# Attention into top-1 experts: min and exp of each step ranked first, row scatters declared independent

## The chip, the cores and the metric

The kernel runs on one core of a Trainium2 chip. The metric is the device time of one execution in microseconds (us), lower is better, median of several runs.

## What is computed

Two stages stand one behind the other. The first is attention with rotary embedding over 4 batches and 8 heads, 576 positions, head size 64. The second is a layer of 8 experts over the 2304 rows of 512 that the attention leaves; every row goes to one expert. Which expert it is hangs on the row before: where the local gate is at least one half, the row takes over the expert of its predecessor.

```python
def _attn_ref(q, k, v):
    q_rot, k_rot = (rotate(q), rotate(k))
    scores = scale * np.matmul(q_rot, k_rot.transpose(0, 1, 3, 2))
    scores = scores - np.max(scores, axis=-1, keepdims=True)
    attn = np.exp(scores)
    attn = attn / (np.sum(attn, axis=-1, keepdims=True) + 1e-09)
    return np.matmul(attn, v).astype(np.float32)

def _moe_ref(x, w_gate, w_local, w1, w2):
    ...
            fresh_e = int(np.argmax(logits[b, s]))
            if s == 0 or local_gate[b, s] < 0.5:
                e = fresh_e
            else:
                e = prev_e if prev_e >= 0 else fresh_e
            ...
            h = np.maximum(x[b, s] @ w1[e], 0.0)
            out[b, s] = p[e] * (h @ w2[e])
```

## The kernel before, in words

**Tiling.** Two heads make a pair, so there are 16 pairs; each pair is cut into 9 steps of 128 queries against 576 keys, and one loop runs over the 144 steps g. Step 9p is pair p's first. From pair 2 on the first step of a pair is the tail tile, which holds the last 64 queries of both heads (its exp writes a tile `et`; the others write `e`). Products that need fp32 are made of two fp32r parts: a high part, cast by ACT, and a low part, the rest, by DVE.

**One step.** The loop's body writes, for step g: the minimum over the scores (`softmax_min`, L269, on DVE: `mn<-s`); the scores of the next step (`mm_s(g + 1)`, L264, on PE); the exp (`softmax_exp`, L286, on ACT: `e<-s,mn` or `et<-s,mn`, with the row sums); the transposes of step g-2 (`tr_main`: PE `tm` L322, two of nine steps also `tk` L332, the tail also `tt` L338), whose result ACT casts (`pth<-tm`, `pkh`, L300) and DVE subtracts (`ptl<-tm,pth`, `pkl`, L304); up to five matmuls of step g-11's product with v (`pv`, L358), whose result is taken out by ACT (`tmp<-pv`, L368) and DVE (`xt<-pv,tmp`, L369). Rope and splits of later pairs go to POOL and the DMA queues. From pair 2 on the gates of a finished pair (PE `gx` L433, DVE `gm` L441 and `xrow` L443) and, around pairs 13 to 15, the routing of three batches (many short operations on DVE: `mx`, `rs`, `d`, `c8`, `key` ...) lie among the steps.

**What is shared.** The scores have two PSUM buffers, so `mm_s(g)` waits until the exp of step g-2 has read its buffer. One pool of four PSUM buffers holds `tm`, `tk`, `tt`, `pv`, `gx` and the small tiles of the routing. The normalising sums are set at a batch's turn (L423, L426).

**What sets the order.** Each step is a region of its own: within it the first 12 steps keep every engine in the order of the code, later steps only PE. How the instructions of neighbouring regions fall among one another, and everything on DVE, ACT, POOL and SP from step 12 on, is the scheduler's choice, which takes the ready instruction with the smallest rank. Behind the loop comes a drain whose order is written out by hand, and then the experts.

**The experts.** 19 tiles of 128 rows run, one behind the other: gather of rows (POOL), transposes, first product (`h`, L918), relu, transposes, second product (`o`, L940), scaling by ACT (`os<-o,x`, L945) and a scatter of the 128 rows to their places in the output, issued by POOL (L946). The scatters go to the same output tensor, and each waits until the one before has landed. Behind the last scatter the program only waits for its landing.

The loop's head is:

```python
                mn = softmax_min(g)
                if g + 1 < NSTEP:
                    mm_s(g + 1)
                softmax_exp(g, mn)
                if g >= 2:
                    tr_main(g - 2)
                pv_steps(g - 11)
```

Of the kernel before, what the change touches and what calls it, by code (L numbers as in the profile page):

```python
# [37 lines left out]
MAN1 = None  # L38
MAN2 = {mybir.EngineType.PE, mybir.EngineType.DVE}
MAN0 = {PE_}  # L40
LOAD0 = 4
ON_POOL = (125, 129, 130, 132, 134)
DRAIN = "tPststatbgttttwtguttegSuuuxXGGGSS"
# [92 lines left out]
def tile_attention_moe(ctx, tc, qk, v, tabs, turn, consts, tri, wg, wts, out):  # L136
    nc = tc.nc
    pe, act, dve, pool, sp = nc.tensor, nc.scalar, nc.vector, nc.gpsimd, nc.sync
# [94 lines left out]
    def spread(p):  # L233
        spread_tail(p)
        spread_k(p)
        spread_q(p)

    def heads_of(i):
        return (i % 2, i // 2)

    def tile_of(g):

        p, i = divmod(g, 9)
        return p, i if p < 2 else (i + 8) % 9

    def mm_s(g):
        p, i = tile_of(g)
        m, q = m_t[p], qst[p % 2]
        st = ps_s.tile([P, 2, 512], F32, tag="s", name=f"s_{g}")
        whole = [(h, 0, HALF, h * HALF) for h in range(2)]  # L250

        turned = [(0, 0, HALF, 64), (1, 0, 224, 64 + HALF), (1, 224, HALF, 0)]
        if i < 8:
            a, j = heads_of(i)
            seq = [(q[:, a, j * P:(j + 1) * P], m[:, a, c], whole) for c in range(2)]
        elif p > 1:
            qt, k = qtail[p % 2], xk[p % 2]
            seq = [(qt[:, x], k[:, y], whole) for x, y in PASSES]
        else:
            seq = [(qtail0[p][:, a], m[:, a, c], (whole, turned)[a]) for a in range(2) for c in range(2)]  # L260
        for h in range(2):
            parts_ = [(lhs, keys, lo, hi, k0) for lhs, keys, parts in seq for hh, lo, hi, k0 in parts if hh == h]
            for n, (lhs, keys, lo, hi, k0) in enumerate(parts_):
                pe.matmul(st[:, h, lo:hi], lhs, keys[:, k0:k0 + hi - lo], start=(n == 0), stop=(n == len(parts_) - 1))  # L264
        s_t[g] = st

    def softmax_min(g):
        mn = sm_p.tile([P, 1], F32, tag="mn", name=f"mn_{g}", bufs=4)
        dve.tensor_reduce(mn, s_t[g][:, :, 0:HALF], axis=AX.XY, op=ALU.min)  # L269
        return mn  # L270

    def softmax_exp(g, mn):
        p, i = tile_of(g)
        b, hp = divmod(p, NP)
        sums = sum_t[b]
        if i < 8:
            a, j = heads_of(i)
            if a == 0:
                e_t[p, j] = ej_p.tile([P, 2, S], F32, tag="ej", name=f"e_{p}_{j}")
            dst = e_t[p, j][:, a]  # L280
            col = (2 * hp + a) * NB + j
        else:
            e_t[p, 4] = et_p.tile([P, S], F32, tag="et", name=f"et_{p}")
            dst = e_t[p, 4]
            col = 2 * hp * NB + 4
        act.activation(  # L286
            dst.rearrange("p (h s) -> p h s", h=2), s_t.pop(g)[:, :, 0:HALF], AF.Exp,
            bias=mn, scale=-1.0, accum_out=sums[:, col:col + 1],
        )
# [414 lines left out]
    def early():  # L704
# [45 lines left out]
        def load_more():  # L750
            for k in range(2, LOAD0):
                load_w(0, k)
            yield
# [65 lines left out]
    def load_w(t, k):  # L819

        if t in regs:
            e, need = regs[t]
            if k == 7 and not w_stage:
                w_stage.append(over.tile([P, 2 * S], F32, tag="xk1", name="stage_7"))
            cols = slice(k * 1024, (k + 1) * 1024)
            sp.dma_start(staged(k), wts[bass.ds(e, 1), :, cols], cond=need)
# [108 lines left out]
    def second_product(t):  # L935
        ps = ps_t.tile([P, 512], F32, tag="t", name=f"o_{t}")
        for k in range(8):
            w = w_t[t, 4 + k // 2]
            for n, (x, y) in enumerate(PASSES):
                pe.matmul(ps, hs_t[t][:, x, k], w[y][:, (k % 2) * 512:(k % 2 + 1) * 512],  # L940
                          start=(k == 0 and n == 0), stop=(k == 7 and n == 2))
            if k % 2 == 1:
                yield k
        o = et_p.tile([P, S], F32, tag="et", name=f"os_{t}")
        act.activation(o[:, 0:DM], ps, AF.Copy, scale=x_t[t][:, DM:DM + 1])  # L945
        pool.indirect_dma_start(  # L946
            out=outf, out_offset=bass.IndirectOffsetOnAxis(ap=sidx[:, t:t + 1], axis=0),
            in_=o[:, 0:DM], in_offset=None, bounds_check=NT - 1, oob_is_err=False)

    LAST = KE + U_LATE - 1  # L950

    def experts_phase():
# [33 lines left out]
        for _ in second_product(LAST):  # L986
            yield LAST
# [122 lines left out]
    if True:  # L1110
# [39 lines left out]
        for g in range(NSTEP):  # L1150
            if g == GM:
                begin.close()
            with tc.manual_schedule(engines=None if g < GM else MAN0):
                p, i = divmod(g, 9)
                if i == 0 and p % NP == 0:
                    b = p // NP
                    sum_t[b] = sm_p.tile([P, H * NB], F32, tag="sum", name=f"sum_{b}")
                    dve.memset(sum_t[b], 1.0)
                mn = softmax_min(g)
                if g + 1 < NSTEP:  # L1160
                    mm_s(g + 1)
                softmax_exp(g, mn)
                if g >= 2:
                    tr_main(g - 2)
                pv_steps(g - 11)

                if i == 0 and 2 <= p and p + 2 < NPAIR or g == SPREAD_LAST:
                    spread(p + 1)
                if g in START:
                    for f in START[g]:  # L1170
                        f()
                if i == 0 and 1 <= p and p + 2 < NPAIR:
                    rope(p + 2)
                    if p + 3 < NPAIR:
                        load_qk(p + 3)
                if i == 5 and 1 <= p and p + 3 < NPAIR:
                    split_qk(p + 2)
                if g == QK_LAST:
                    split_qk(NPAIR - 1)
                if i == 3 and 1 <= p and p + 1 < NPAIR:  # L1180
                    split_v(p + 1)
                    if p + 2 < NPAIR:
                        load_v(p + 2)

                if i == GATES_AT.get(p, 7) and p >= 2:
                    soon += gates(p - 2)
                    if (p - 2) % NP == NP - 1:
                        soon.append(lambda b=(p - 2) // NP: scores(b))
                        if (p - 2) // NP == B - 2:
                            todo += route(0, B - 1)  # L1190
                if soon:
                    soon.pop(0)()
                f = todo.pop(0) if todo else None
                if f:
                    list(f())
        moe = experts_phase()
        with tc.manual_schedule(engines=MAN1):
# [20 lines left out]
            def rest_of_w():  # L1218
                for k in range(LOAD0, 8):
                    load_w(0, k)  # L1220
# [81 lines left out]
```

## Time and profile before

| what | value |
|---|---|
| time, median of 3 runs | 553.76 us (553.4 to 555.82) |
| the profiled execution, its own time | 553.2 us |
| its span, first to last instruction | 551.0 us |
| mean granted TensorE clock | 0.993 |
| PE, matmuls | 525.8 us busy (95%) |
| PE, weight loads | 465.9 us busy (85%) |
| DVE | 383.7 us busy (70%) |
| ACT | 339.5 us busy (62%) |
| POOL | 326.4 us busy (59%) |

The page gives busy time over the whole span. The stages differ: the attention runs from about 13 to 294 us, the drain to about 320, the experts to 540, and the rest is the last scatter and the end of the program. What a stage is bound by is read from its own stretch. In a row of the timeline the first number is the start, the second the length; the bracket at the end gives the idle time of that engine just before the row and what ended it.

### The profile page before, as it was taken

What the parts mean: (1) busy time and instruction counts of PE and PEld (TensorE: products, weight loads), DVE (VectorE), ACT (ScalarE), POOL (GpSimd) and SP (SyncE); (2) the same over time, 40 slices, a digit from 0 to 9 for tenths busy, and PEclk for the clock granted to TensorE, in tenths of its full rate; (3) what the DMA queues carried; (4) which work ended last, traced back from release to release, by engine and by line L of the source; (5) the groups of instructions that cost most, each with busy time, mean ns of one, the idle gap of its engine ahead of it and who ended that gap; (6) DMA issues with size and microseconds to landing.
All of it is one profiled execution on the core that took longest, in us unless ns stands there. A gap on an engine that the chain in (4) does not pass through costs nothing. (4 is left out here: it accounts for less than half of the span.)

```text
span 551.0 us, 10813 instructions
## 1 busy us (share of the span) xinstructions
PE 525.8 (95%) x3328; PEld 465.9 (85%) x3329; DVE 383.7 (70%) x723; ACT 339.5 (62%) x755; POOL 326.4 (59%) x243
## 2 busy tenths in 40 slices
PE   7989999999999999998999999999999999999991
PEld 3788999999999999997888788887888888888881
DVE  5898999999999999999999746356411545312530
ACT  2989889888998999987667424252422344423340
POOL 2995988989778788985698202265312444411331
PEclk9999999999999999999999999999999999999997
DMA  8558597886787787886298224644215464215140
GB/s 282 217 117 214 176 252 204 188 228 191 215 229 176 202 229 208 216 199 160 29 187 239 68 50 143 207 176 163 69 39 204 131 259 167 82 39 192 58 136 24
DMA packets 48774, 90.46 MB, mean 164 GB/s; under 512 B 15233, under 2 KB 25473, under 8 KB 46914
## 3 DMA queue, kind: packets, MB, share of 16 engines
q1 hardware_dynamic: 45666, 79.96, 51.2%
q0 software_dynamic: 3040, 9.71, 5.5%
q8 instruction: 29, 0.48, 0.4%
q14 instruction: 39, 0.32, 0.2%
HBM read 109.95 MB, written 9.71 MB: 217 GB/s over the span
## 5 line engine op out<-in xcount | busy, mean ns | idle before, releaser
L940 PE MATMUL o<-w,hs 128*128 128x512 f32 x456 | 113.1, 398 | 0.0
L269 DVE TENSOR_REDUCE mn<-s 128x1 f32<-128x576 f32 x144 | 107.4, 746 | 4.2 <-PE s L264 2.7
L918 PE MATMUL h<-w,xs 128*128 128x512 f32 x444 | 106.1, 392 | 0.8 <-DVE xs L304 0.5
L286 ACT ACTIVATE e<-s,mn 128x576 f32<-128x576 f32 x128 | 95.3, 745 | 17.3 <-DVE mn L269 14.3
L264 PE MATMUL s<-m,qst 128*128 128x288 f32 x512 | 97.6, 311 | 5.9 <-ACT e L286 3.7
L946 POOL DMA_INDIRECT out_dram<-os,sidx x19 | 22.8, 1198 | 132.2 <-ACT os L945 84.4
L304 DVE TENSOR_TENSOR ptl<-tm,pth 128x512 fp32r<-128x512 f32 x139 | 95.0, 684 | 6.3 <-ACT pth L300 4.1
L918 PEld LDWEIGHTS h<-w,xs 128*128 128x128 f32 x444 | 82.5, 188 | 19.0 <-DVE w L866 1.1
L940 PEld LDWEIGHTS o<-w,hs 128*128 128x128 f32 x456 | 83.1, 188 | 16.9 <-DVE hs L304 0.4
L300 ACT CAST pth<-tm 128x512 fp32r<-128x512 f32 x139 | 81.0, 582 | 12.9 <-PE tm L322 12.0
L264 PEld LDWEIGHTS s<-m,qst 128*128 128x128 f32 x512 | 74.6, 188 | 12.4 <-ACT e L286 6.1
L322 PE MATMUL tm<-wid,e 128*128 128x128 f32 x512 | 76.9, 272 | 0.9 <-ACT e L286 0.5
L358 PE MATMUL pv<-pth,v 128*128 128x288 f32 x256 | 76.4, 314 | 0.4 <-DVE ptl L304 0.2
L358 PE MATMUL pv<-ptl,v 128*128 128x288 f32 x256 | 76.5, 314 | 0.0
L193 POOL TENSOR_TENSOR stage<-stage 128x1152 f32<-128x1152 f32 x26 | 69.0, 2668 | 11.7 <-DMA stage<-in_qk_dram 9.0
L866 DVE TENSOR_TENSOR w<-stage,w 128x1024 fp32r<-128x1024 f32 x41 | 56.0, 1404 | 25.4 <-POOL w L865 13.7
L322 PEld LDWEIGHTS tm<-wid,e 128*128 128x128 f32 x512 | 62.0, 140 | 1.6 <-ACT e L286 0.7
L304 DVE TENSOR_TENSOR hs<-th,hs 128x512 fp32r<-128x512 f32 x38 | 24.6, 685 | 42.7 <-ACT hs L300 40.1
L304 DVE TENSOR_TENSOR xs<-tx,xs 128x512 fp32r<-128x512 f32 x19 | 13.1, 689 | 58.0 <-ACTq L872 48.0
L358 PEld LDWEIGHTS pv<-pth,v 128*128 128x128 f32 x256 | 48.2, 188 | 2.9 <-DVE ptl L304 0.9
L300 ACT CAST xs<-tx 128x512 fp32r<-128x512 f32 x19 | 11.1, 586 | 61.8 <-PE tx L904 61.7
L358 PEld LDWEIGHTS pv<-ptl,v 128*128 128x128 f32 x256 | 48.3, 189 | 0.0
(191 smaller groups left out, 827.8 us busy)
## 6 DMA issues: line engine op xcount, KB each, us to landing
stage<-in_wts_dram SPq DMA_DIRECT2D x152, 512.0 KB
stage<-in_qk_dram SPq DMA_DIRECT2D x13, 1152.0 KB
qst<-xq SPq DMA_DIRECT2D x56, 128.0 KB
stage<-in_v_dram SPq DMA_DIRECT2D x16, 320.0 KB
m<-xq SPq DMA_DIRECT2D x14, 288.0 KB
m<-xk SPq DMA_DIRECT2D x14, 288.0 KB
m<-xq SPq DMA_DIRECT2D x14, 256.0 KB
m<-xk SPq DMA_DIRECT2D x14, 256.0 KB
```

What stands on the lines that cost most here:

```text
L193: engine.tensor_tensor(x, x, tab[:, 2 * f:2 * f + 2], op=ALU.mult)
L264: pe.matmul(st[:, h, lo:hi], lhs, keys[:, k0:k0 + hi - lo], start=(n == 0), stop=(n == len(parts_) - 1))
L269: dve.tensor_reduce(mn, s_t[g][:, :, 0:HALF], axis=AX.XY, op=ALU.min)
L286: act.activation(dst.rearrange("p (h s) -> p h s", h=2), s_t.pop(g)[:, :, 0:HALF], AF.Exp, bias=mn, scale=-1.0, accum_out=sums[:, col:col ...
L300: act.copy(hi, src)
L304: dve.tensor_tensor(lo, src, hi.bitcast(F32), op=ALU.subtract)
L322: pe.transpose(ps[:, k], src[:, k * P:(k + 1) * P], ident)
L358: pe.matmul(pv_t[p, u], lhs.rearrange("p c d -> p (c d)"), rhs, start=(n == 0), stop=(n == 9))
L866: (pool if k in on_pool else dve).tensor_tensor(lo, src, hi.bitcast(F32), op=ALU.subtract)
L918: pe.matmul(ps[:, c], xs_t[t][:, x, k], w[y][:, c * 512:(c + 1) * 512], start=(k == 0 and n == 0), stop=(k == 3 and n == 2))
L940: pe.matmul(ps, hs_t[t][:, x, k], w[y][:, (k % 2) * 512:(k % 2 + 1) * 512], start=(k == 0 and n == 0), stop=(k == 7 and n == 2))
L946: pool.indirect_dma_start(out=outf, out_offset=bass.IndirectOffsetOnAxis(ap=sidx[:, t:t + 1], axis=0), in_=o[:, 0:DM], in_offset=None, bou ...
```

## The change

It has two parts. First, the minimum and the exp of every step are written inside a block that takes 400 off their rank, so that the scheduler places them as if they stood that much earlier in the code. Second, each row scatter is declared to have no dependence on the other row scatters, since their rows differ. No instruction is added, taken away or made different; the order on the engines and the waits differ. Below, line numbers of the changed kernel are higher by one (helpers) up to four (loop).

```diff
+SOON = 400
...
         o = et_p.tile([P, S], F32, tag="et", name=f"os_{t}")
         act.activation(o[:, 0:DM], ps, AF.Copy, scale=x_t[t][:, DM:DM + 1])
-        pool.indirect_dma_start(
+        done = pool.indirect_dma_start(
             out=outf, out_offset=bass.IndirectOffsetOnAxis(ap=sidx[:, t:t + 1], axis=0),
             in_=o[:, 0:DM], in_offset=None, bounds_check=NT - 1, oob_is_err=False)
+
+        tc.declare_no_dep(done.ins, group="rows out", reason="rows of their own")
+        tc.add_to_no_dep_group("rows out", done.ins)
...
-                mn = softmax_min(g)
+
+                with tc.high_priority(offset=SOON):
+                    mn = softmax_min(g)
                 if g + 1 < NSTEP:
                     mm_s(g + 1)
-                softmax_exp(g, mn)
+                with tc.high_priority(offset=SOON):
+                    softmax_exp(g, mn)
                 if g >= 2:
                     tr_main(g - 2)
```

On ACT, around the border from pair 7 to pair 8 (steps 70 to 73; `e_7_3` are exps of pair 7, `et_8` is the tail tile that opens pair 8, `e_8_0` the next step's exp), the order before is:

```order
L300 CAST pth_7_2244<-tm_68_2394 128x4x128
L368 COPY tmp_6_2292<-pv_6_2_2376 64x288
L286 ACTIVATE e_7_3_2392,sum_1_1284<-s_71_2387,mn_71_2415 128x576
L300 CAST pth_7_2244<-tm_69_2425 128x4x128
L426 ACTIVATE sum_1_1284<-sum_1_1284 128x10
L286 ACTIVATE et_8_2452,sum_2_2443<-s_72_2417,mn_72_2445 128x576
L300 CAST pth_7_2244<-tm_70_2454 128x4x128
L423 COPY sum_2_2443<-sum_2_2443 64x1
L286 ACTIVATE e_8_0_2503,sum_2_2443<-s_73_2447,mn_73_2496 128x576
```

and with the change, at the same place:

```order
L301 CAST pth_7_2244<-tm_68_2394 128x4x128
L287 ACTIVATE e_7_3_2392,sum_1_1284<-s_71_2387,mn_71_2415 128x576
L369 COPY tmp_6_2292<-pv_6_2_2376 64x288
L427 ACTIVATE sum_1_1284<-sum_1_1284 128x10
L301 CAST pth_7_2244<-tm_69_2425 128x4x128
L301 CAST pth_7_2244<-tm_70_2454 128x4x128
L287 ACTIVATE e_8_0_2503,sum_2_2443<-s_73_2447,mn_73_2496 128x576
L287 ACTIVATE et_8_2452,sum_2_2443<-s_72_2417,mn_72_2445 128x576
L424 COPY sum_2_2443<-sum_2_2443 64x1
```

The exp of step 71 has moved ahead of the copy `tmp_6`; the exp of the tail tile has moved from ahead of the second cast to behind it, and behind the exp of step 73.

On DVE, where the routing of three batches begins (`mx_3`, `rs_7`, `d_4`, `c8_6`, `f_8`, `key_9`) among the steps 125 to 128, the order before is:

```order
L304 TENSOR_TENSOR ptl_13_3980<-tm_123_4179,pth_13_3979 128x4x128
L485 TENSOR_REDUCE mx_3_4211<-lg_all_110 128x15
L498 SCALAR_TENSOR_TENSOR rs_7_4219<-lg_all_110,cst_90 128x15
L427 RECIPROCAL sum_3_3601<-sum_3_3601 128x10
L488 TENSOR_TENSOR d_4_4213<-lg_all_110,mx_3_4211 128x120
L269 TENSOR_REDUCE mn_127_4228<-s_127_4191 128x1
L496 SCALAR_TENSOR_TENSOR c8_6_4217<-d_4_4213,cst_90 128x120
L304 TENSOR_TENSOR ptl_13_3980<-tm_124_4198,pth_13_3979 128x4x128
L501 TENSOR_REDUCE f_8_4221<-c8_6_4217 128x15
L564 TENSOR_REDUCE se_10_4270<-ex_5_4215 128x15
L504 TENSOR_TENSOR key_9_4223<-rs_7_4219,f_8_4221 128x15
L269 TENSOR_REDUCE mn_128_4277<-s_128_4230 128x1
```

and with the change:

```order
L305 TENSOR_TENSOR ptl_13_3980<-tm_123_4179,pth_13_3979 128x4x128
L270 TENSOR_REDUCE mn_127_4228<-s_127_4191 128x1
L305 TENSOR_TENSOR ptl_13_3980<-tm_124_4198,pth_13_3979 128x4x128
L270 TENSOR_REDUCE mn_128_4277<-s_128_4230 128x1
L486 TENSOR_REDUCE mx_3_4211<-lg_all_110 128x15
L499 SCALAR_TENSOR_TENSOR rs_7_4219<-lg_all_110,cst_90 128x15
L428 RECIPROCAL sum_3_3601<-sum_3_3601 128x10
L489 TENSOR_TENSOR d_4_4213<-lg_all_110,mx_3_4211 128x120
L497 SCALAR_TENSOR_TENSOR c8_6_4217<-d_4_4213,cst_90 128x120
L502 TENSOR_REDUCE f_8_4221<-c8_6_4217 128x15
```

Both minima have moved ahead of the routing's operations.

On PE, at the start of pair 2's product with v (`pv_1_0` is the first of pair 1's four parts; `s_22` and `s_23` are scores of pair 2), the order before is:

```order
L322 MATMUL tm_18_801<-wid_93,et_2_716 128x128 x4
L338 MATMUL tt_18_808<-wid_93,et_2_716 128x128
L264 MATMUL s_22_825<-m_2_445,qst0_99 128x288 x4
L358 MATMUL pv_1_0_814<-pth_1_521,v2_1_420 128x288
L358 MATMUL pv_1_0_814<-ptl_1_522,v2_1_420 128x288
```

and with the change:

```order
L323 MATMUL tm_18_801<-wid_93,et_2_716 128x128 x4
L265 MATMUL s_22_825<-m_2_445,qst0_99 128x288
L339 MATMUL tt_18_808<-wid_93,et_2_716 128x128
L265 MATMUL s_22_825<-m_2_445,qst0_99 128x288 x3
L265 MATMUL s_23_857<-m_2_445,qst0_99 128x288 x4
L359 MATMUL pv_1_0_814<-pth_1_521,v2_1_420 128x288
```

The scores of step 23 have moved ahead of all ten matmuls of `pv_1_0`.

## Rows read from the trace of the kernel before

**Rows 1.** Busy time per stretch: stretch, length, engines with instructions, clock, DMA share, GB/s

```profile
96.00:116.00 20.00, 19.76 (x155) 19.25 (x154) 19.05 (x38) 17.31 (x45) 17.33 (x12) 1.00 0.79 217
...
196.00:216.00 20.00, 20.00 (x160) 19.77 (x159) 19.41 (x38) 18.69 (x47) 17.79 (x12) 1.00 0.76 194
...
320.00:540.00 220.00, 219.49 (x1085) 181.13 (x1084) 89.71 (x128) 77.71 (x109) 75.11 (x56) 1.00 0.39 133
```

**Rows 2.** Waits of PE's weight loads for scores: total us, times, longest

```profile
PEld s L264 <- ACT e L286: 6.1, 9, 1.3
...
PEld s L264 <- ACT et L286: 3.8, 8, 0.7
```

**Rows 3.** Timeline of PE at four pair borders: start, us, what, idle before

```profile
134.71 0.81 PE L264 MATMUL s<-m,qst 128*128 128x288 f32 x4 [0.24 <-ACT et L286]
...
151.24 0.78 PE L264 MATMUL s<-m,qst 128*128 128x288 f32 x4
...
168.24 0.80 PE L264 MATMUL s<-m,qst 128*128 128x288 f32 x4 [0.24 <-ACT et L286]
...
184.76 0.79 PE L264 MATMUL s<-m,qst 128*128 128x288 f32 x4
```

**Rows 4.** Timeline of ACT ahead of a border with a stall (scores at 100.79)

```profile
99.41 0.59 ACT L300 CAST pth<-tm 128x512 fp32r<-128x512 f32 x1 [1.02 <-PE tm L322]
99.89 0.75 ACT L286 ACTIVATE et<-s,mn 128x576 f32<-128x576 f32 x1
```

**Rows 5.** Timeline of ACT ahead of the border at 151.24, without a stall

```profile
149.40 0.74 ACT L286 ACTIVATE et<-s,mn 128x576 f32<-128x576 f32 x1
...
150.37 0.59 ACT L300 CAST pth<-tm 128x512 fp32r<-128x512 f32 x1
```

**Rows 6.** Timeline of PE, stalls of pairs 0 to 2

```profile
24.45 0.66 PE L264 MATMUL s<-m,qst 128*128 128x288 f32 x3 [1.04 <-ACT e L286]
30.84 0.81 PE L264 MATMUL s<-m,qst 128*128 128x288 f32 x4 [0.48 <-ACT et L286]
33.01 0.80 PE L264 MATMUL s<-m,qst 128*128 128x288 f32 x4 [0.71 <-ACT e L286]
34.71 0.80 PE L264 MATMUL s<-m,qst 128*128 128x288 f32 x4 [0.35 <-ACT e L286]
...
53.06 0.80 PE L264 MATMUL s<-m,qst 128*128 128x288 f32 x4 [0.45 <-ACT e L286]
```

**Rows 7.** Timeline of ACT, the exp of step 21

```profile
53.97 0.74 ACT L286 ACTIVATE e<-s,mn 128x576 f32<-128x576 f32 x1
```

**Rows 8.** Timeline of DVE where the routing of three batches begins

```profile
250.54 1.38 DVE L498 SCALAR_TENSOR_TENSOR rs<-lg_all,cst 128x15 f32<-128x15 f32 x1
...
252.11 0.75 DVE L269 TENSOR_REDUCE mn<-s 128x1 f32<-128x576 f32 x1
```

**Rows 9.** Timeline of PE in the routing stretch, its two longest stalls

```profile
253.79 0.80 PE L264 MATMUL s<-m,qst 128*128 128x288 f32 x4 [0.98 <-ACT e L286]
...
268.26 1.04 PE L264 MATMUL s<-xk,qtail 128*128 128x288 f32 x6 [0.86 <-issue]
```

**Rows 10.** Busy time in the whole routing stretch, columns as in rows 1

```profile
246.00:294.00 48.00, 43.62 (x331) 39.00 (x330) 46.33 (x112) 34.71 (x85) 36.61 (x43) 1.00 0.68 143
```

**Rows 11.** The chain that ended last: start, us, what

```profile
538.27 4.08 issue
```

**Rows 12.** Timeline of ACT, the scalings of the last two tiles

```profile
535.20 0.68 ACT L945 ACTIVATE os<-o,x 128x512 f32<-128x512 f32 x1
539.84 0.69 ACT L945 ACTIVATE os<-o,x 128x512 f32<-128x512 f32 x1 [3.96 <-PE o L940]
```

**Rows 13.** Timeline of POOL, the last two scatters

```profile
536.15 2.12 POOL L946 DMA_INDIRECT out_dram<-os,sidx  x1 [3.37 <-ACT os L945]
542.55 0.98 POOL L946 DMA_INDIRECT out_dram<-os,sidx  x1 [4.28 <-issue]
```

**Rows 14.** Line of the scatters: its semaphore waits, shortest/median/longest ns

```profile
L946 POOLq EVENT_SEMAPHORE  x19: 17/17/5828, 328.4 to 536.0; - x19
```

## The prediction

> **What bounds the kernel now.** I read the busy times by stretch first. In the steady attention the matmuls take 19.76 to 20.00 of 20 us and DVE 19.05 to 19.41 [rows 1]: PE is the bound, with DVE hardly behind it, and ACT (17.3 to 18.7) has a little room. In the experts PE takes 219.49 of 220 us [rows 1], and neither part of the change moves anything there but scatters, so that stretch is taken as unchanged. What can be won is the idle time of PE in the attention and the end behind the last matmul. The view of waits prices the first: the weight loads of the scores wait 6.1 us for exps of ordinary steps and 3.8 us for exps of tail tiles [rows 2], some 10 us or 1.8% of the span. That is the ceiling of putting min and exp first, if nothing else became late.
>
> Three places hold that idle time. First the pair borders: at 134.71 and 168.24 the scores wait for the tail tile's exp (the matmul row shows 0.24 us idle, the start of the whole pair moves by more: 16.53 us from 134.71 to 151.24, where no stall stands, 17.00 us on to 168.24, where one does, 16.52 us on to 184.76, without) [rows 3]. So one border stall costs 0.47 us. The same bracket stands at the starts of pairs 3 to 7 and 9, six in all; pairs 8 and 10 and the later ones have none. Second, pairs 0 to 2, with stalls of 1.04, 0.48, 0.71, 0.35 and 0.45 us [rows 6]. Third, the routing stretch from 246 to 294 us, where PE is busy 43.62 of 48 us and DVE 46.33 [rows 10]: there DVE is the bound.
>
> The chain that ended last is short and holds the end: 4.08 us in which POOL's last scatter stands still [rows 11].
>
> **The scatters.** Each scatter waits until the one before has landed. The semaphore waits on that line are 17 ns at the median and 5828 ns at most [rows 14]: only the last one matters. The scatter before it started at 536.15, 0.27 us behind the end of its scaling (535.20 + 0.68) [rows 12, 13]. The last scaling ended at 540.53 (539.84 + 0.69), but its scatter started at 542.55 [rows 12, 13]. Without the wait it should start 0.27 behind the scaling, at 540.80, which is 1.75 us earlier, and all that follows hangs on its landing. Against that stands the neighbour, whose data are then still in flight (its 5.83 us wait began near 536.0 and so ended near 541.8), and the 0.7 us from that end to the start at 542.55, part of which may stay. Taking half of that 0.7 as kept gives about 1.4; **term: -1.5 us**, from -1.0 to -1.8. No gain in other scatters: their waits are 17 ns.
>
> **The borders.** At the borders with a stall ACT first does the two casts of `tm`, standing idle 1.02 us for the second (cast at 99.41), and only then the tail exp at 99.89 [rows 4]. At 151.24 the tail exp stands ahead of the second cast, at 149.40, the cast at 150.37 [rows 5], and PE has no gap. The printed order of the change puts both casts, and the next step's exp too, ahead of the tail exp at the start of pair 8. The rank would suggest the opposite; but the scheduler places what is ready by its own clock, so a smaller rank doesn't keep an exp ahead of a cast which was ready before it. The two score buffers then change roles, so the next scores wait for the exp that comes first, which starts behind the cast: 150.37 + 0.59, about 151.0, ending about 151.7, against scores that started at 151.24 [rows 3, 5]. That is the 0.5 us which the other borders show. The same order stands at pair 10, and at pairs 4 to 7 and 9 the casts stay ahead, as before. So the six stalls stay and two are added: **term: 2 x 0.47 = +0.9 us**. The bounds: 0, if the swapped buffer comes free as early as now, down to -2.8 (6 x 0.47) if the earlier minima let all six vanish, and up to +1.9 if pairs 11 and 12 get it as well (4 x 0.47).
>
> A rule speaks against any effect here. The Trainium skill, "Perfetto Trace Analysis", section "Identifying Performance Opportunities", says that a gap that repeats on the engine which should be saturated can mean too few SBUF or PSUM buffers for the next tile. By it the two score buffers would cause the border stall, order would neither make nor mend it, and the sum would be lower by this term's 0.9 us. The trace disagrees: the same two buffers serve the start at 151.24 without a gap [rows 3].
>
> **Inside the pairs.** The minima stand ahead of `xt`, `pkl` and the gates on DVE, so some 0.3 to 0.6 us earlier each (a `ptl` or an `xt` is that long). But PE has no gap there: 20.00 of 20 us in pairs 11 to 13 [rows 1]. What is pulled ahead delays what frees the shared PSUM buffers, by one exp at most (0.75 us [rows 4]). **Term: -0.3 us** over the eleven pairs 3 to 13, between the ends -0.9 and +4.4 (0.4 us per pair, the slower rival).
>
> **Pairs 0 to 2.** Four stalls up to 34.71 make 2.58 us [rows 6]. There the first 12 steps keep each engine in the order of the code within a step, so only neighbouring steps can overlap; exps that pass a cast win at one step and the casts behind them lose it at the next. I take nothing, between -2.6 and +1.0 (one more stall like the largest). In pair 2 the stall of 0.45 at 53.06 can go, but the scores of step 23 now stand ahead of the whole of `pv_1_0`. They are due at 53.7 (four matmuls behind 53.06) and need the exp of step 21, which ran from 53.97 to 54.71 [rows 7]: up to 1.0 us of wait where five products with v ran before. With a minimum that comes half a us earlier the wait is 0.5 and the stall ahead of it shrinks a little: +0.3, between -0.45 and +1.0. **Term: +0.3 us**.
>
> **Routing stretch.** The minimum of step 127 stands at 252.11 behind a `rs` of 1.38 us and its neighbours [rows 8]; PE then waits 0.98 us at 253.79 [rows 9]. With the change the minimum stands ahead of them, and this stall goes. But the same DVE work has to be done, DVE has only 48 - 46.33 = 1.67 us of idle time in the stretch [rows 10], and the routing's matmuls and the casts' low parts, which PE needs as well, come later by what was pulled ahead. I take -0.98 for this stall and give 0.8 of it back: **term: -0.2 us**. The ends are -4.4 (all of PE's idle time, 48 - 43.62, with DVE work pushed behind the last minimum) and +1.8 (another pair of stalls like 0.98 and 0.86 [rows 9]).
>
> **Sum.** -1.5 + 0.9 - 0.3 + 0.3 - 0.2 = -0.8 us. The profiled execution took 553.2 us, so 552.4; its own time lies 0.56 us under the median of the runs, and the forecast for a median is 552.8 us, between the two scales.
>
> **Rivals.** *A, the ranking does its work.* The early minima let the exps come early, the six border stalls vanish (-2.8), the stalls at 253.79 and 53.06 go without being given back (-1.4), and the scatter gives 1.5: 553.5 - 5.7 = 547.8 us. For it: all these waits end with an exp [rows 2]. Against it: at the borders the exp isn't late for its rank but stands behind casts, which the new order keeps. *B, slower.* At each pair an exp passes a copy of `pv` or a cast (the printed order shows `tmp_6` behind the exp of step 71), so a shared PSUM buffer comes free 0.75 us later and PE, which has no room in pairs 3 to 13, waits. It decides from where PE's next use of that buffer stands less than 0.75 us behind its release now. At 0.4 us per pair over eleven pairs: +4.4, with the borders' 0.9 and the scatter's -1.5: 553.5 + 3.8 = 557.3 us. For it: 20.00 of 20 us [rows 1]; against it: the copies' buffers are four, and ACT and DVE have gaps in every pair. *C, the ranking changes nothing that PE sees*, and only the scatter counts: 553.5 - 1.5 = 552.0 us.
>
> **How the numbers follow.** Forecast 0.47, A 0.29, B 0.12, C 0.12. A measurement of this kernel tells about 0.5% from no change, 2.8 us: faster is below 551.0, slower above 556.5. A lies below; of the forecast and of C I give 0.06 to below it, through the routing stretch; B lies above, and the forecast's ends hold 0.01 of it. So faster 0.35, same 0.52, slower 0.13. The range for 8 in 10 leaves out the lower third of A and most of B: 547.4 to 556.8; the forecast's own range is 550.5 to 555.
>
> **What would show it.** In the changed profile the last scatter should start about 0.3 us behind its scaling, with no wait on that line over 1 us. The waits of scores for tail exps should be eight rather than six borders, with pairs 8 and 10 at some 17.0 us; if they are gone, A is right. A wait of `s` near 53.7 for the exp of step 21 should be new, and the 0.98 at 253.79 gone, with later waits of `pv` or the routing's matmuls for DVE in its place. A PE below 19.7 us per 20 in 196 to 236 would be B. I would be wrong by the sum if PE's idle time in 246 to 294 fell by more than 1.7 us.

## The result, and the profile after

The changed kernel is slower: 557.57 us median against 553.40 in nine runs each, a ratio of 1.0087 (95% interval 1.0067 to 1.0108), some 4.2 to 4.8 us. The profiled execution took 558.09 us, its span is 556.2 us.

Five views of its trace answer to the rows ahead of the prediction. First the timeline of PE at the starts of pairs 7 to 10 (as [rows 3]):

```profile
134.78 0.80 PE L265 MATMUL s<-m,qst 128*128 128x288 f32 x4 [0.24 <-ACT e L287]
...
151.67 0.80 PE L265 MATMUL s<-m,qst 128*128 128x288 f32 x4 [0.24 <-ACT e L287]
...
168.59 0.80 PE L265 MATMUL s<-m,qst 128*128 128x288 f32 x4 [0.24 <-ACT e L287]
...
185.49 0.81 PE L265 MATMUL s<-m,qst 128*128 128x288 f32 x4 [0.24 <-ACT e L287]
```

The starts at 151.67 and 185.49 now have the border stall which 151.24 and 184.76 had not.

Second, PE in pair 2 (as the last of [rows 6]):

```profile
51.58 0.40 PE L265 MATMUL s<-m,qst 128*128 128x288 f32 x1 [0.39 <-ACT e L287]
...
53.70 0.80 PE L265 MATMUL s<-m,qst 128*128 128x288 f32 x4 [1.20 <-ACT e L287]
```

The wait of 0.45 us has become 0.39 and 1.20; the exp that the second one waits for started on ACT at 52.81:

```profile
52.81 0.74 ACT L287 ACTIVATE e<-s,mn 128x576 f32<-128x576 f32 x1
```

Third, PE at the middle of pair 11, and DVE and ACT at the same place (pairs 12 and 13 look the same); nothing waited there before. The last two rows are busy times: from 196 to 236 us PE is no longer full, 19.66 of 20 us where it had 20.00 [rows 1]:

```profile
205.83 0.37 PE L359 MATMUL pv<-pth,v 128*128 128x288 f32 x1 [0.20 <-DVE pkl L305]
```

```profile
203.80 0.69 DVE L305 TENSOR_TENSOR ptl<-tm,pth 128x512 fp32r<-128x512 f32 x1
204.59 0.76 DVE L270 TENSOR_REDUCE mn<-s 128x1 f32<-128x576 f32 x1
205.27 0.41 DVE L305 TENSOR_TENSOR pkl<-tk,pkh 128x256 fp32r<-128x256 f32 x1
```

```profile
203.82 0.74 ACT L287 ACTIVATE e<-s,mn 128x576 f32<-128x576 f32 x1
...
204.55 0.36 ACT L301 CAST pkh<-tk 128x256 fp32r<-128x256 f32 x1
```

```profile
196.00:216.00 20.00, 19.66 (x155) 19.12 (x154) 18.91 (x39) 17.85 (x45) 17.13 (x12) 1.00 0.75 195
216.00:236.00 20.00, 19.66 (x156) 19.13 (x154) 18.94 (x38) 17.89 (x47) 16.56 (x11) 1.00 0.85 238
```

Fourth, the end of the attention: PE's longest stall of the whole trace, then DVE and POOL just ahead of it, then the busy times with the granted clock (the number behind POOL's):

```profile
294.16 0.63 PE L323 MATMUL tm<-wid,e 128*128 128x128 f32 x4 [1.89 <-DVE gm L442]
```

```profile
290.81 1.94 DVE L650 TENSOR_TENSOR ex<-c,cst 128x90 bf16<-128x90 bf16 x1
292.67 0.74 DVE L270 TENSOR_REDUCE mn<-s 128x1 f32<-128x576 f32 x1
293.34 0.35 DVE L651 TENSOR_SCALAR ex<-c,cst 128x90 bf16<-128x90 bf16 x1
293.60 0.41 DVE L305 TENSOR_TENSOR pkl<-tk,pkh 128x256 fp32r<-128x256 f32 x1
293.93 0.18 DVE L442 TENSOR_TENSOR gm<-gx,sum 128x36 f32<-128x36 f32 x1
```

```profile
290.27 2.37 POOL L837 TENSOR_TENSOR w_m<-stage,w_m 128x1024 fp32r<-128x1024 f32 x1
292.61 1.04 POOL L836 TENSOR_SCALAR w_q<-stage 128x1024 fp32r<-128x1024 f32 x1
```

```profile
292.00:294.00 2.00, 0.27 (x3) 0.03 (x1) 2.00 (x5) 0.77 (x2) 1.92 (x3) 1.00 1.11 342
294.00:296.00 2.00, 1.84 (x12) 1.86 (x13) 1.97 (x6) 1.26 (x4) 2.00 (x1) 0.81 0.88 308
296.00:298.00 2.00, 2.00 (x24) 1.86 (x23) 0.81 (x4) 0.39 (x1) 0.12 (x1) 0.50 0.78 178
```

PE does 0.27 us of work in two, and behind that the clock stands at half (1.2 of 2.4 GHz) for some 3 us. Fifth, the last scatters on POOL (as [rows 13, 14]):

```profile
541.89 2.11 POOL L947 DMA_INDIRECT out_dram<-os,sidx  x1 [3.38 <-ACT os L946]
546.58 0.98 POOL L947 DMA_INDIRECT out_dram<-os,sidx  x1 [2.57 <-ACTq L998]
```

```profile
L947 POOLq EVENT_SEMAPHORE  x17: 17/17/43, 349.9 to 541.7; - x17
```

The last scaling ended at 546.31, so its scatter starts 0.27 us behind it instead of 2.02.

**Where the time went.** The same steps can be compared between two traces. The table takes the starts of the scores of steps 0, 18, 27, 99, 127 and 143 and of the first product of the experts' second tile, and gives for each stretch by how many us it is longer than in the trace of the kernel before. The last column is the measured ratio.

```
                      0-18  18-27  27-99  99-127 127-143  143-     sum   ratio
                            pair 2 3-10   11-13  routing  drain
changed kernel        0.15  1.23   0.45   1.88   1.04     2.05    6.80  1.0087
scatter alone         0.02  0.01  -0.02   0.02   0.23     0.00    0.26  0.9976
ranking alone         0.16  2.45   0.45   1.94   1.11     2.10    8.21  1.0133
minimum alone         0.49  1.24  -0.03  -0.11   3.97     3.53    9.09  1.0151
exp alone             0.12  0.03   0.15   1.05  -0.03    -0.12    1.20  1.0025
ranked up to 125      0.15  1.24   0.39   1.89   0.00    -0.05    3.62  1.0056
ranked from 126       0.01  0.00   0.00   0.03   0.77     5.30    6.11  1.0059
ranked up to 141      0.80  1.23   0.49   1.90   1.12    -0.34    5.20  1.0048
tk ranked too         0.13  1.10   1.11  -0.12   2.64    -0.53    4.33  1.0093
borders turned        0.23  0.02  -0.41   0.09  -0.07    -0.01   -0.15  0.9967
27-141, tk too        0.66 -0.02   1.05  -0.16   3.99    -1.21    4.31  1.0064
changed, ex on POOL   0.15  1.24   0.51   1.88   1.10     0.27    5.15  1.0064
27-141, ex on POOL    0.04  0.03   1.01  -0.12   0.14     0.76    1.86  1.0022
scatter, ex on POOL   0.00  0.00  -0.02   0.05   2.76     0.55    3.34  1.0044
```

All rows but the ranking, the minimum and the exp alone contain the independent scatters, whose gain lies behind the last column of stretches.

Each row is one profiled execution, while the ratio is that of all runs: the executions of the kernel ranked up to 125 (553.76 us) and of the one with `tk` ranked too (554.08) are the second lowest and the lowest of their runs, that of the kernel ranked up to 141 (558.45) is the highest of its. The stretch ahead of step 0 is not in the sum; it lasted from 10.7 to 13.9 us in these executions. The 0.80 and 0.66 of the first column stand beside a granted clock of 0.50 for some 3 us from 12.0 and 11.7 us on, which no other of these traces has.

### The profile page after: what moved, and what is told of

It is laid out like the page before. It is cut to its first block, busy times and chain, and to the rows that moved or that the text cites. A ratio compares the mean times of both kernels' runs of the same rounds, so it can differ in the third digit from the quotient of the medians.

```text
span 556.2 us, 10828 instructions
## 1 busy us (share of the span) xinstructions
PE 528.2 (95%) x3328; PEld 466.7 (84%) x3329; DVE 384.2 (69%) x723; ACT 338.7 (61%) x755; POOL 326.7 (59%) x243
## 4 chain that ended last, share of the span: by engine, by line
PE 74%; DVE 9%; ACT 6%; issue 4%; POOL 2%; DMA 1%; SPq 1%; POOLq 0%; DVEq 0%; ACTq 0%
PE h L919 17%; PE o L941 16%; PE s L265 12%; PE pv L359 12%; PE tm L323 9%; DVE mn L270 3%; PE th L932 3%; ACT e L287 2%; ACT pth L301 2%; PE gx L434 2%; PE tx L905 1%; DVE ptl L305 1%; DVE w L867 1%; PE tk L333 1%; DMA stage<-in_qk_dram 1%
## 5 line engine op out<-in xcount | busy, mean ns | idle before, releaser
L265 PEld LDWEIGHTS s<-m,qst 128*128 128x128 f32 x512 | 75.1, 188 | 12.7 <-ACT e L287 10.7
L323 PE MATMUL tm<-wid,e 128*128 128x128 f32 x512 | 78.2, 275 | 3.0 <-DVE gm L442 1.9
```

The lines of the kernel that those rows point to most:

```text
L323: pe.transpose(ps[:, k], src[:, k * P:(k + 1) * P], ident)
```

## The experiments

**Each part alone.** Scatters alone:

```diff
-                with tc.high_priority(offset=SOON):
-                    mn = softmax_min(g)
+                mn = softmax_min(g)
...
-                with tc.high_priority(offset=SOON):
-                    softmax_exp(g, mn)
+                softmax_exp(g, mn)
```

> Only the scatters are declared independent; the ranking is as before, and the order on PE, DVE and ACT is that of the kernel before. Theory M (the whole loss is the ranking's): the last scatter starts 0.27 us behind its scaling instead of 2.02, the attention is unchanged, the time falls by 0.6 to 1.75 us, 551.7 to 552.8 against 553.4. Rival S (the scatters cost, since two in flight land later): the scatter starts early but its landing comes as late as before or later, and the time is equal or up to 1 us longer.

Measured: 550.94 against 551.87 us, ratio 0.9976 (0.9962 to 0.9991), 1.3 us faster. The attention is the same to 0.3 us; the last scatter starts at 540.80 where it had started at 542.55:

```profile
536.15 2.12 POOL L947 DMA_INDIRECT out_dram<-os,sidx  x1 [3.37 <-ACT os L946]
540.80 0.98 POOL L947 DMA_INDIRECT out_dram<-os,sidx  x1 [2.52 <-ACTq L998]
```

So this part gains, and the ranking costs more than the whole loss. The ranking alone (the two lines on the scatter taken out):

> Only the ranking of minimum and exp; the scatters wait for one another as before. Theory M: the attention and the drain are those of the changed kernel (pair 2 +1.2 us, borders 8 and 10 +0.4 each, pairs 11 to 13 +0.6 each, routing and drain +3 or more), and the last scatter waits again: slower than the changed kernel by 0.6 to 1.75 us, so 558.2 to 559.3, some +5 to +6 against before. Rival S: as fast as the changed kernel or faster, 556.5 to 557.6.

Measured: ratio 1.0133 (1.0102 to 1.0163), +7.3 us, more than the 5 to 6 expected. In its profiled execution the clock fell behind the stall of 1.21 us in pair 2 as well, and that column is twice that of the changed kernel. Minimum only, then exp only (one of the two blocks taken out):

> Only the minimum is ranked first, not the exp; scatters as before. Its printed order has the tail exp behind both casts at pairs 8 and 10, the scores of step 23 ahead of the product with v, and the last minimum ahead of the gates, but the pk cast and subtraction of pairs 11 to 13 where they were. Theory M: pair 2 +1.2, borders 8 and 10 +0.4 each, no loss in pairs 11 to 13, the 1.9 us stall near 294 stays: +3 to +5 us, 556.5 to 558.5. Rival X (the exps on ACT do the harm, the minima are harmless): within 1 us of before.

> Only the exp is ranked first, not the minimum; scatters as before. Its printed order leaves pairs 2, 8 and 10 as before and has the exp ahead of the pk cast in pairs 11 to 13, with the scores of the next step ahead of the product with v. Theory M: +0.6 us in each of pairs 11 to 13, nothing at pairs 2, 8, 10: +1.5 to +2.5 us, 555 to 556. Rival X: nearly all of the loss, +4 us or more.

Measured: minimum alone 1.0151 (1.0128 to 1.0174), +8.3 us; exp alone 1.0025 (1.0012 to 1.0038), +1.4. The exps do a little harm, and exactly in pairs 11 to 13; pair 2 comes from the minima. But the minima alone cost more than both together, and nearly all of it in routing and drain (3.97 and 3.53 us), more than expected. That they would there do more harm than the whole was not in the theory; the trace has both of the collisions told below (`code` 3.00 us, `ex` 2.28). Pair 8 got its border stall (0.50 us), pair 10 did not, and pairs 3 to 10 cost nothing in all (-0.03), where 0.4 us at each of the two was expected.

**Stretches of the ranking.** The block's offset was made to hang on the step:

```diff
-                with tc.high_priority(offset=SOON):
+                with tc.high_priority(offset=SOON if 0 <= g < 126 else 0):
```

> The changed kernel with the ranking in steps 0 to 125 only; steps 126 to 143 are ranked as before, scatters independent. Theory P (three places add up): the scatter gives -1.3, pair 2 costs 1.2, borders 8 and 10 together 0.4 net of the small gains inside the pairs, pairs 11 to 13 some 1.4 to 1.9, routing and drain nothing: +1.5 to +2.5 us against before. Rival Q (nearly all of the loss arises in routing and drain): within 0.7 us of the kernel with independent scatters alone, so 1 us or more below before.

> The changed kernel with the ranking in steps 126 to 143 only, scatters independent. Theory P: in the changed kernel's trace the stretch from step 126 to the first expert adds 4.0 us, of which 1.9 us is one stall near 292 and some 1.5 us the granted clock of 0.50 behind it; with the scatter's -1.3 that gives +2 to +3.5 us against before. Rival Q: +4.5 us or more. Rival N (the stretch is bound by DVE's work, and the order of it costs nothing): -1.3 us.

> The changed kernel with steps 142 and 143 ranked as before; its printed order has the gates' multiplication and rows of pair 13 ahead of the last minimum again. Theory P with the clock: the 1.9 us stall of the transposes near 294 goes, and with it the stretch at a granted clock of 0.50 behind it: 2.5 to 3.5 us faster than the changed kernel. Rival without the clock: 1.9 us faster at most, and the clock falls all the same. Rival N: no difference, another wait takes the place.

Measured: steps 0 to 125 only, 1.0056 (1.0036 to 1.0076), +3.1 us, more than the 1.5 to 2.5 expected; steps 126 to 143 only, 1.0059 (1.0038 to 1.0081), +3.3; steps 0 to 141, 1.0048 (1.0029 to 1.0067), +2.7, so by the ratios 2.1 faster than the changed kernel, a little less than expected. The front's columns are those of the changed kernel to 0.1 us, and behind step 126 nothing is lost in its trace. The rival with everything in routing and drain falls. But the two parts don't add up to the whole: without the scatters' 1.3 us they cost 4.4 and 4.6, which is 9.0 against 6.1 for the changed kernel and 7.3 for the ranking alone. The back alone loses 5.30 us in the drain where the changed kernel loses 2.05, with a stall of 2.62 us and some 7 us at a granted clock of 0.50. With steps 142 and 143 ranked as before the drain's loss is gone (-0.34) and the clock stays at 1.00 there. That looked like a proof that the last minimum's place ahead of the gates makes the stall.

**The small transposes ranked too.** In `tr_main`:

```diff
-            split_to(pkhi[p][:, cs], pklo[p][:, cs], ps[:, 0:256])
+            with tc.high_priority(offset=SOON):
+                split_to(pkhi[p][:, cs], pklo[p][:, cs], ps[:, 0:256])
```

> The changed kernel, and in addition the cast and the subtraction of the small transposes tk ranked first like the exp; its printed order has pkl ahead of the next minimum again in pairs 11 to 13, and no scores moved ahead of the product with v there. Theory P (a shared PSUM buffer held by tk until pkl has run): the waits of pv for pkl, 0.2 us on the row and 0.6 us per pair at pairs 11 to 13, are gone, and the one of 1.41 us near 258.7 shrinks: 1.5 to 3 us faster than the changed kernel. Rival: the product with v waits for the next thing in the buffer's row and the pairs still take 0.6 us more each: no difference.

Measured: the loss in pairs 11 to 13 is gone (-0.12 against 1.88). The product with v runs without a wait, with `pkl` ahead of the minimum again:

```profile
204.17 0.27 PE L340 MATMUL tt<-wid,et 128*128 128x128 f32 x1
204.31 0.37 PE L360 MATMUL pv<-pth,v 128*128 128x288 f32 x1
```

But the time is not: 1.0093 (1.0067 to 1.0118), with single runs from 554.1 to 560.6 us and their mean clocks from 0.994 to 0.985. The order behind step 126 came out differently, and the routing column rose from 1.04 to 2.64; there, too, `code` took 3.02 us, with a PE stall of 2.17 behind it.

**The borders turned.** On top of the scatters alone, and without any ranking of minimum or exp (LATE is pairs 3 to 7 and 9):

```diff
                 if g >= 2:
-                    tr_main(g - 2)
+                    with tc.high_priority(offset=-60 if i == 0 and p in LATE else 0):
+                        tr_main(g - 2)
```

> The kernel before with independent scatters and, in the first step of pairs 3 to 7 and 9, the cast and subtraction of the transposes ranked 60 later (no ranking of minimum and exp). Its printed order has the tail tile's exp ahead of the second cast at every pair, as pairs 8 and 10 have it in the kernel before. Theory P (a border stall is the place of the tail exp behind that cast): the six stalls at the starts of pairs 3 to 7 and 9 vanish, 6 times 0.47 us, with the scatter's -1.3: 3.5 to 4.1 us below before. Rival (two score buffers cause it, or the late cast frees its PSUM buffer later by as much): no more than the scatter's -1.3, or a new wait of pv or tm in the same pairs.

Measured: 550.80 us, ratio 0.9967 (0.9949 to 0.9984), 1.8 us below before; so beyond the scatters no more than 0.5 us, which the intervals don't separate. The stall is gone at every border, here at the start of pair 5, but three or four steps on there is another:

```profile
100.14 0.79 PE L265 MATMUL s<-m,qst 128*128 128x288 f32 x4
...
103.59 0.40 PE L265 MATMUL s<-m,qst 128*128 128x288 f32 x1 [0.26 <-ACT e L287]
```

Against the kernel before, pair 5's start gains 0.50 us (step 46 to step 47) and gives 0.4 back by step 52. So the border stall is the place of the tail exp behind the cast, as the prediction said, but taking it away is worth little: six stalls of 0.50 us went, and pairs 3 to 10 together became 0.41 us shorter.

**Three places taken back.** Ranking in steps 27 to 141 only, `tk` ranked in the same steps:

> The changed kernel with three of its four costly places taken back: ranking only in steps 27 to 141 (so pair 2 and the last two steps are ranked as before), and the small transposes' cast and subtraction ranked with the exps. The tail exps still stand behind both casts at pairs 3 to 10. Theory P (pair 2, pairs 11 to 13 and the last minimum are the rest of the loss): 5 to 6 us faster than the changed kernel, that is 0 to 1.5 us below before, with a stall at pairs 8 and 10. Rival (the loss is spread, or moves to the next waits): 2 us or more above before.

Measured: 1.0064 (1.0044 to 1.0085), +3.5 us, where 0 to -1.5 was expected. Pair 2 (-0.02) and pairs 11 to 13 (-0.16) are clean, the borders cost 1.05, and a stall like the drain's has come back earlier (routing 3.99), though the last minimum stands where it stood before the change. The theory of the last minimum falls with this. What the traces of the two kernels have in common stands on DVE and POOL. Here DVE, then POOL, in this kernel:

```profile
284.42 3.00 DVE L696 SCALAR_TENSOR_TENSOR code<-code,cst 128x6 f32<-128x6 f32 x1
287.35 1.28 DVE L305 TENSOR_TENSOR ptl<-tm,pth 128x512 fp32r<-128x512 f32 x2
```

```profile
283.94 0.73 POOL L210 TENSOR_SCALAR v<-stage 128x640 fp32r<-128x640 f32 x1
284.63 1.28 POOL L298 TENSOR_TENSOR ptl<-stage,pth 128x512 fp32r<-128x512 f32 x1
285.87 1.53 POOL L211 TENSOR_TENSOR v<-stage,v 128x640 fp32r<-128x640 f32 x1
```

```profile
288.17 1.06 PE L323 MATMUL tm<-wid,e 128*128 128x128 f32 x4 [2.16 <-DVE ptl L305]
```

An addition of 128x6 numbers takes 3.00 us: it starts beside the first of these operations of POOL's and ends at 287.42, when the third ends (287.40). In the kernel before it took 0.17. The row of PE is the stall behind it. In the changed kernel `ex` takes 1.94 and ends at 292.75, POOL's at 292.64. In the kernel ranked up to 141, where the drain loses nothing, `ex` starts only 0.18 us before one of POOL's operations ends, and ends 0.10 behind it (DVE, then POOL):

```profile
292.89 0.27 DVE L650 TENSOR_TENSOR ex<-c,cst 128x90 bf16<-128x90 bf16 x1
293.09 0.24 DVE L651 TENSOR_SCALAR ex<-c,cst 128x90 bf16<-128x90 bf16 x1
```

```profile
290.32 1.60 POOL L211 TENSOR_TENSOR v<-stage,v 128x640 fp32r<-128x640 f32 x1
292.01 1.06 POOL L836 TENSOR_SCALAR w_m<-stage 128x1024 fp32r<-128x1024 f32 x1
293.15 2.41 POOL L837 TENSOR_TENSOR w_m<-stage,w_m 128x1024 fp32r<-128x1024 f32 x1
```

The new theory: DVE's short operations stand still beside POOL's long ones; the order decides which of them meet, and that is what makes the stall.

**The collision taken away.** `ex` made on POOL itself, in the changed kernel; then `ex` and `code`, in the kernel just above; then both in the kernel with the scatters alone. In the second cut `lead` is left out on POOL, where it is zero:

```diff
-            dve.tensor_tensor(rhs[:, 0], w, bc(C["tok64"][:, 0:nblk], 2, n), op=ALU.mult)
-            dve.tensor_scalar(rhs[:, 1], w, C["p1"], None, op0=ALU.mult)
+            (pool if first == 0 else dve).tensor_tensor(rhs[:, 0], w, bc(C["tok64"][:, 0:nblk], 2, n), op=ALU.mult)
+            (pool if first == 0 else dve).tensor_scalar(rhs[:, 1], w, C["p1"], None, op0=ALU.mult)
```

```diff
-        dve.scalar_tensor_tensor(c, c, lead, C["tile128"][:, 0:n], op0=ALU.add, op1=ALU.add)
+        if n == KE:
+            pool.tensor_tensor(c, c, C["tile128"][:, 0:n], op=ALU.add)
+        else:
+            dve.scalar_tensor_tensor(c, c, lead, C["tile128"][:, 0:n], op0=ALU.add, op1=ALU.add)
```

> The changed kernel with the two short operations that make ex in the routing of three batches moved from DVE to POOL; the orders on PE and ACT are those of the changed kernel word for word, DVE's too but for the two. In the changed kernel's trace ex took 1.94 us on DVE (290.81 to 292.75) and ended with POOL's subtraction of a weight (290.27 to 292.64); in a run without such an overlap the same operation took 0.27 us. Theory D (DVE stands still while POOL's long operation on SBUF runs, and the 1.89 us stall of PE behind it comes from that): the stall near 294 and the stretch at a granted clock of 0.50 behind it vanish: 2.5 to 4 us faster than the changed kernel, 0.1 to 0.4% over before. Rival (the last minimum's place ahead of the gates makes the stall): 0.5 us faster at most.

> The earlier kernel with three of the four places taken back (h1_rest), and ex and the addition that makes code on POOL as well. There code took 3.00 us on DVE (284.42 to 287.42) and ended with POOL's operation (287.40), with PE standing still for 2.16 us. Theory D: that stall and the fall of the clock behind it go, 3 to 4.5 us faster than h1_rest, 0 to 1.5 us below before. Rival: POOL's queue now delays code and the stall stays: within 1 us of h1_rest.

> The kernel with independent scatters alone, and ex and code on POOL. In the kernel before ex took 1.00 and 0.86 us on DVE, beside POOL's operations, code 0.17. Theory D: DVE gains some 1.4 us in a stretch that it bounds, PE's stalls near 274, 285 and 292 shrink by up to 1 us in all: 0 to 1 us faster than the kernel with independent scatters alone, 1.3 to 2.3 below before. Rival: no difference to it, or slower if code waits in POOL's queue.

Measured in the first: the order on PE and ACT is the changed kernel's, the last minimum stands ahead of the gates as there, and the 1.89 us stall is gone, with the clock at 1.00 through the attention and the drain; the drain's column falls from 2.05 to 0.27. DVE, then PE at the place of that stall:

```profile
292.87 0.74 DVE L270 TENSOR_REDUCE mn<-s 128x1 f32<-128x576 f32 x1
293.53 0.18 DVE L442 TENSOR_TENSOR gm<-gx,sum 128x36 f32<-128x36 f32 x1
```

```profile
293.83 0.60 PE L323 MATMUL tm<-wid,e 128*128 128x128 f32 x4
```

Two other waits of PE appear, 0.51 (for `ex` on POOL) and 0.82 (for a `ptl`). The ratio is 1.0064 (1.0039 to 1.0089), 1.3 us better than the changed kernel: the direction is theory D's, the size about half of the least that it allowed, and the intervals of the two overlap. The move also takes `ex` off DVE altogether, so this run alone shows that the stall hangs on `ex`; that POOL made `ex` long is read from where the rows end. The second: 1.0022 (1.0006 to 1.0038), 2.3 us better than without the move, where 3 to 4.5 was expected, and still above before. In its trace a conversion meets POOL instead, and PE then waits 1.94 us. DVE, POOL, PE:

```profile
292.31 2.16 DVE L667 CAST gidx<-ihi 128x6 uint32<-128x6 f32 x1
```

```profile
292.09 2.35 POOL L841 TENSOR_TENSOR w_q<-stage,w_q 128x1024 fp32r<-128x1024 f32 x1
```

```profile
295.40 0.40 PE L360 MATMUL pv<-pth,v 128*128 128x288 f32 x1 [1.94 <-DVE ptl L305]
```

The third is the rival's: 1.0044 (1.0018 to 1.0070), slower than the kernel with the scatters alone. There `code` had met nothing (0.17 us on DVE); now it stands in POOL's queue, DVE waits 3.94 us for it, and PE stands still for 3.50:

```profile
287.54 0.61 PE L265 MATMUL s<-m,qst 128*128 128x288 f32 x1 [3.50 <-ACT e L287]
```

## Why the prediction was wrong

Its forecast was -0.8 us, and its whole range (to 556.8) lay below the result. Term by term:

- **The scatters were right.** Term -1.5, measured -1.3 alone; start 0.27 us behind the scaling as written.
- **The borders were right.** Pairs 8 and 10 got the stall, the six others kept theirs: the steps from 73 to 74 and from 91 to 92 became 0.50 us longer each, against 2 x 0.47. With the small gains inside pairs 3 to 10 the stretch is only 0.45 longer in all, so half of the term was given back.
- **Inside the pairs the sign was wrong for three of them.** The term was -0.3; pairs 11 to 13 cost 1.88 (0.63 each), 1.05 to 1.9 of it the exps' doing. It is rival B's mechanism at another place: it was priced for `tmp` in every pair and happens with `tk` in three. The exp runs ahead of the `pkh` cast (204.55 instead of directly behind the high part), the next minimum ahead of `pkl`, and the product with v can't open until `pkl` has freed its PSUM buffer. Ranking `tk` with them took exactly this away. The prediction's own sign for B, PE below 19.7 of 20 us, came with it (19.66). That B's 557.3 us lies beside the measured 557.57 is luck all the same: of its 4.4 us inside the pairs 1.88 came, in three pairs, and the rest arose in pair 2, routing and drain, which B left alone.
- **Pair 2 was mis-sized.** The scores of step 23 do stand ahead of the product with v and wait for the exp of step 21. But I expected 0.5 us of wait, since the minimum comes earlier; it waited 1.20, because ACT did a copy and two casts first (the exp started at 52.81, 0.97 us behind the end of its minimum). The waits of 0.39 and 1.20 are 1.14 us more than the 0.45 before, and the pair came out 1.23 longer, beyond the upper end of 1.0.
- **Routing and drain were the step that failed.** The term was -0.2, the end +1.8; measured +3.1 in the profiled execution (1.04 and 2.05). The 0.98 us stall at 253.79 did go, and more than that was given back: `pkl` now stands behind the routing's operations, and the product with v waits for it.

```profile
258.69 0.37 PE L359 MATMUL pv<-pth,v 128*128 128x288 f32 x1 [1.41 <-DVE pkl L305]
```

What was missing: I added up DVE's operations with the durations of the trace before, and took order as the only thing that changes. But `ex`, 1.00 us there (a smaller collision already, its 284.38 lies 0.11 behind the end of one of POOL's operations), took 1.94 beside POOL's subtraction, and the 1.89 us stall that followed was paid a second time by the clock. The drain was not in the sum at all. The run with `ex` on POOL shows that the last minimum's rank alone does not make that stall: the minimum stands ahead of the gates there too, and with `ex` off DVE the stall is gone.
- **Rival A** had nothing: the waits of the weight loads for exps rose from 9.9 [rows 2] to 12.4 us. Those for ordinary exps grew from 6.1 to 11.4; part of that only changed its name, since the scores at the borders now wait for an ordinary exp where they had waited for the tail's:

```profile
PEld s L265 <- ACT e L287: 11.4, 19, 1.4
...
PEld s L265 <- ACT et L287: 1.0, 3, 0.5
```

The rule of the Trainium skill that was weighed, on repeated gaps and buffers ("Perfetto Trace Analysis", section "Identifying Performance Opportunities"), is answered by the run with the borders turned: with the same two score buffers the stall is gone at all borders, so order made it there. But most of it came back within a few steps, and whether more buffers would win that, no run here shows.

What stays open: in which runs the clock falls, and so what the drain costs on average; and why the scatter's landing takes one of two times (below).

## What to carry to other kernels

A rank is not an order: the scheduler fills each engine by its own idea of when things are ready, so an exp "first in rank" still stood behind casts, and what it did pass was the cast that frees a shared buffer. When an order is changed on an engine that is full, look first at which instruction frees the next buffer that PE opens, and don't carry durations of short DVE operations over to an order in which they stand beside other POOL work. Of a change in two parts time each alone: here one gained 1.3 us and the other lost some 7.

## What the runs showed of the hardware

**DVE beside POOL.** Eight short DVE operations lasted until 0.02 to 0.11 us behind the end of one of POOL's, in seven traces: `ex` 1.94, 1.95, 1.91 and 2.28 us, `code` 3.00, 3.00 and 3.02, and the conversion `gidx` 2.16. The shortest times of the same operations were 0.27, 0.15 and 0.17. The Trainium skill ("SBUF — State Buffer", section "Who interferes with whom") says that DVE and GpSimd share a pair of SBUF ports, that a DVE operation with two SBUF inputs contends with a GpSimd operation that reads SBUF, and that the later of the two is blocked until the other ends. The four of `ex`, which reads two tensors, agree. `code` does so in part: all three times it began beside one of POOL's operations and outlasted the next two as well, and in five other traces it took 0.15 to 0.17 us inside one of POOL's 0.6 us operations that make `ohr`. `gidx` has one input, so that sentence does not cover it.

**The clock beside a stall.** In or behind PE stalls of 1.9 to 3.5 us near the end of the attention the granted clock went to 0.50, for 3 to 7 us, in the changed kernel and in five of the experiments (ranking alone, minimum alone, ranked from 126, 27 to 141 with `tk`, scatter with `ex` on POOL). In two others it did not fall (2.17 us with `tk` ranked too, 1.94 in the second kernel with `ex` on POOL). The stall of 1.2 to 1.4 us in pair 2 was followed by a fall in one trace of seven (the ranking alone). The kernel of the scatters with `ex` on POOL, which has such a stall, spread by 7 us from run to run (551.9 to 558.9), the one with the scatters alone by 3.2. But the kernel ranked up to 125, whose trace has no such stall behind step 126, spread by 6.1 (553.3 to 559.3), so that the falls make the spread is not shown.

**Two landings.** With independent scatters the time from the last scatter's issue to its landing was 2.8 us in four traces and 3.7 to 4.2 in seven; with the wait it was 3.0 to 3.1 in the four that have it. So 0.6 to 1.2 us of the 1.75 gained at the start is lost again in more than half of the profiled executions.
